# A fused attention and two-network kernel: the second network's first matrix two blocks at a time, in seven products instead of eight

## The chip, the cores and the metric

One Trainium2 chip, one core. The metric is the device time of one execution in microseconds (us). TensorE is called PE here, its weight loads PEld, VectorE is DVE, ScalarE is ACT, GpSimd is POOL, SyncE is SP.

## What is computed

```python
def _attn_ref(q, k, v):                 # [8, 8, 576, 64], chunks of 64
    scores = scale * np.matmul(q_c, k_c.transpose(0, 1, 2, 4, 3))
    scores = scores - np.max(scores, axis=-1, keepdims=True)
    attn = np.exp(scores)
    attn = attn / (np.sum(attn, axis=-1, keepdims=True) + 1e-09)
    out = np.matmul(attn, v_c)
...
def _moe_ref(x, w_gate, w_val, w_out, rms_g):      # first network, 512 -> 1536 -> 512
    xn = x / np.sqrt(np.mean(x * x, axis=-1, keepdims=True) + 1e-06) * rms_g
    g = xn @ w_gate
    silu = g * (1.0 / (1.0 + np.exp(-g)))
    return silu * (xn @ w_val) @ w_out
def _moe2_ref(x, w_in, w_out):                     # second network, 512 -> 2048 -> 512
    h = x @ w_in
    g = h * np.clip(h + 3.0, 0.0, 6.0) / 6.0
    return g @ w_out
```

The attention's output, 4608 tokens of 512 values, goes through the first network and then through the second. Everything is float32. The weights of both networks come as pairs of 32-bit words that are put together on the chip.

## The kernel before

The tokens form nine blocks of 512 columns (N), with the 512 features in four parts of 128 (KD = 4). For the matmuls each float32 operand is held as a high part, rounded to the PE's format, and a low part, the rest. A product of two operands is then three matmuls: high by high, low weight by high, high weight by low. The block of a network's input stands in XH and XL (high and low, four tiles of 128x512 each).

The first network runs block after block, 12 steps f each (FA). Between its matmuls two hooks issue other work: att_hook the attention of the block that comes next, prep_hook the preparation of weights. In blocks 1 to 8 of the first network, prep_hook takes four tiles of the second network's weights per block through Stash: load on ACT's queue, put together and split in high and low (ACT, DVE, POOL), store to DRAM on ACT's queue. In the last block all 32 tiles are fetched on SP's queue into the pool wp, 36 buffers of 128x2x512, where they stay. The first network's output goes to DRAM as well (yd, one tensor per block).

The second network, again block after block, has 16 steps f (FB) per block. A step has 12 matmuls of mm_up (L598), which make 128 rows of h in one PSUM bank, then relu on ACT (L813), gate on DVE (L814), split_act (the cast on ACT, L636, and the subtraction on POOL, L637), and 12 matmuls of mm_down_b (L615, L616, L619) with the activations of the step before into four PSUM banks. So the elementwise work of a step lies beside the matmuls of the next. At a block's start load_x2 brings the next block's input from yd in one 1 MB DMA (L661), and ahead of the last mm_down_b x_split splits it (casts L587 on ACT, subtractions L589, two on DVE and two on POOL). o_store (L651, L657) drains the four banks, ACT and DVE in turn, and writes them out.

The order of the instructions on each engine is the order in which the program issues them (manual_schedule); waits come from the tiles' dependencies and from how many buffers a pool has: 4 for tmp, 2 each for ah, al and st, 1 each for sg and xf.

Of the kernel before, what the change touches and what calls it, by code (L numbers as in the profile page):

```python
# [43 lines left out]
def fused_kernel(  # L44
# [20 lines left out]
    N = 512  # L65
# [4 lines left out]

    const = ctx.enter_context(tc.tile_pool(name="const", bufs=1))
# [123 lines left out]
    class Stash:  # L195


        def __init__(self, piece):
            self.piece = piece
            self.d = dr_p.tile([128, 2, 512], F32, name=f"stash_{piece[0]}{piece[1]}")  # L200

        def load(self):
            t = st_p.tile([128, 1024], U32, tag="st", name="sraw")
            o = t if self.piece[0] == "out2" else t.rearrange("p (k f) -> p k f", k=KD)
            nc.scalar.dma_start(out=o, in_=w_src(*self.piece))
            t = t.rearrange("p (n w) -> p n w", w=2)
            self.lw, self.hw = t[:, :, 0], t[:, :, 1]
# [10 lines left out]
        def split(self):  # L218
# [6 lines left out]
            self.lo = tmp_p.tile([128, 512], F32R, tag="tmp", name="slo")  # L225
            nc.scalar.copy(self.c.bitcast(F32R), self.lw.bitcast(F32))
            nc.gpsimd.tensor_tensor(self.lo, self.lw.bitcast(F32), self.c.bitcast(F32), op=ALU.subtract)

        def store(self):
            nc.scalar.dma_start(out=self.d[:, 0, :], in_=self.c.bitcast(F32))  # L230
            nc.scalar.dma_start(out=self.d[:, 1, :], in_=self.lo.bitcast(F32))

        def fetch(self):
            w = wp.tile([128, 2, 512], F32R, tag="w", name="w")
            nc.sync.dma_start(out=w.bitcast(F32), in_=self.d)
            W[self.piece] = w
# [344 lines left out]
    XH = xn_p.tile([128, KD, N], F32R, name="XH")  # L581
    XL = xn_p.tile([128, KD, N], F32R, name="XL")
# [9 lines left out]
    def mm_up(bank, w, xs):  # L592
# [19 lines left out]
    def mm_down_b(w, a, first, last, in_turn=False):  # L612
        def high(m):
            am = a[0][:, m * 128:(m + 1) * 128]
            nc.tensor.matmul(PS[:, YB + m, :], am, w[:, 0, :], start=first, stop=False)  # L615
            nc.tensor.matmul(PS[:, YB + m, :], am, w[:, 1, :], start=False, stop=False)  # L616

        def low(m):
            nc.tensor.matmul(PS[:, YB + m, :], a[1][:, m * 128:(m + 1) * 128], w[:, 0, :], start=False, stop=last)  # L619
# [27 lines left out]
    def o_store(b):  # L647
# [206 lines left out]
```

## Time and profile before

| | us |
|---|---|
| median of 3 runs | 1827.24 (1826.59 to 1827.74) |
| the profiled execution | 1826.32 |
| its span in the profile | 1824.5 |
| PE busy | 1766.5 (97% of the span) |
| DVE busy | 643.2 (35%) |
| ACT busy | 601.3 (33%) |
| POOL busy | 491.4 (27%) |

The span runs from the first to the last instruction of the profile; 1.8 us of the profiled execution lie around it. Up to about 84 us the attention of block 0 and the first weights are prepared, to 1036 us the first network runs, from 1036 us the second, with 87.04 us per block. Busy shares are means over all of it. What a group of instructions is worth is read in its own stretch.

### The profile page before, as it was taken

The page shows a single profiled execution, that of the slowest core. Times are in us where ns is not written, and L with a number is a line of the kernel's source. Part 1 is how long each engine was busy: PE and PEld are TensorE (multiplying, and loading weights), DVE is VectorE, ACT ScalarE, POOL GpSimd, SP SyncE. Part 2 cuts the span into 40 slices and gives each one's busy share as a digit, 9 for nine tenths or more (in the row PEclk, how much of TensorE's full clock was granted, in tenths as well). Part 3 has the DMA queues.
Part 4 walks back from the last instruction along what each step waited for, and adds up shares of the span by engine and source line. Part 5 has one row for each costly group of instructions (what it writes and reads, how often), then busy time and mean ns, then how long its engine had stood idle before and what let it go on. Part 6 is the DMA issues. An engine that isn't in the chain of part 4 may idle for free.

```text
span 1824.5 us, 24078 instructions
## 1 busy us (share of the span) xinstructions
PE 1766.5 (97%) x9856; PEld 1451.4 (80%) x9856; DVE 643.2 (35%) x858; ACT 601.3 (33%) x899; POOL 491.4 (27%) x359
## 2 busy tenths in 40 slices
PE   4689999999999999999999999999999999999998
PEld 4567788888888888888888888888888888888887
DVE  7886444454354445435432212121212121212111
ACT  5453333333333333333332223222323232223222
POOL 2321322232222223222222223232323232323222
PEclk7799999999999999999999999999999999999999
DMA  9831232323323242332237501010101010101000
GB/s 261 227 67 32 74 93 71 91 71 82 81 70 94 66 93 74 81 82 70 70 139 253 174 1 47 0 47 0 47 1 47 1 47 1 47 1 47 0 24 24
DMA packets 238000, 127.45 MB, mean 70 GB/s; under 512 B 193472, under 2 KB 213952, under 8 KB 236736
## 3 DMA queue, kind: packets, MB, share of 16 engines
q1 hardware_dynamic: 217920, 92.34, 19.4%
q10 hardware_dynamic: 19968, 33.56, 5.4%
q8 instruction: 77, 1.26, 0.3%
q14 instruction: 35, 0.29, 0.1%
HBM read 90.18 MB, written 35.65 MB: 69 GB/s over the span
## 4 chain that ended last, share of the span: by engine, by line
PE 91%; DVE 3%; DMA 2%; SPq 2%; issue 1%; ACT 1%; POOL 0%; DVEq 0%
PE PS L598 51%; PE PS L619 7%; PE PS L615 7%; PE PS L616 7%; PE PS L607 5%; PE PS L608 5%; PE PS L610 5%; PE PS L474 1%; DMA wraw<-in_moe_w_out_dram 1%; PE PS L534 1%; PE PS L516 1%; DVE kT L462 1%; SPq L265 0%; SPq L132 0%; DVE w L170 0%
## 5 line engine op out<-in xcount | busy, mean ns | idle before, releaser
L598 PE MATMUL PS<-XH,w 128*128 128x512 f32 x2880 | 721.5, 393 | 11.6 <-ACT sg L782 4.1
L637 POOL TENSOR_TENSOR al<-sg,ah 128x512 fp32r<-128x512 f32 x252 | 338.1, 1342 | 1216.1 <-ACT ah L636 1176.9
L598 PEld LDWEIGHTS PS<-XH,w 128*128 128x128 f32 x2880 | 543.2, 189 | 128.1 <-ACT sg L782 4.9
L598 PE MATMUL PS<-XL,w 128*128 128x512 f32 x1440 | 387.3, 391 | 0.0
L814 DVE SCALAR_TENSOR_TENSOR sg<-sg,PS 128x512 f32<-128x512 f32 x144 | 99.3, 689 | 635.5 <-ACT sg L813 635.5
L598 PEld LDWEIGHTS PS<-XL,w 128*128 128x128 f32 x1440 | 271.8, 189 | 57.9 <-POOL XL L400 0.6
L636 ACT CAST ah<-sg 128x512 fp32r<-128x512 f32 x252 | 156.3, 620 | 397.0 <-DVE sg L787 250.2
L813 ACT ACTIVATE sg<-PS,three 128x512 f32<-128x512 f32 x144 | 99.2, 689 | 452.5 <-PE PS L598 439.9
L616 PE MATMUL PS<-w,ah 128*128 128x512 f32 x576 | 224.1, 389 | 0.0
L615 PE MATMUL PS<-w,ah 128*128 128x512 f32 x576 | 224.1, 389 | 0.0
L787 DVE TENSOR_TENSOR sg<-sg,PS 128x512 f32<-128x512 f32 x108 | 74.2, 687 | 403.6 <-PE PS L598 399.6
L607 PE MATMUL PS<-ah,w 128*128 128x512 f32 x432 | 174.8, 405 | 0.0
L608 PE MATMUL PS<-ah,w 128*128 128x512 f32 x432 | 168.3, 390 | 0.0
L619 PE MATMUL PS<-w,al 128*128 128x512 f32 x576 | 154.4, 389 | 0.0
L619 PEld LDWEIGHTS PS<-w,al 128*128 128x128 f32 x576 | 108.1, 188 | 22.8 <-POOL al L637 0.4
L615 PEld LDWEIGHTS PS<-w,ah 128*128 128x128 f32 x576 | 108.1, 188 | 22.4
L616 PEld LDWEIGHTS PS<-w,ah 128*128 128x128 f32 x576 | 108.1, 188 | 22.4
L782 ACT ACTIVATE sg<-PS 128x512 f32<-128x512 f32 x108 | 64.6, 598 | 176.8 <-PE PS L598 159.8
L610 PE MATMUL PS<-al,w 128*128 128x512 f32 x432 | 115.6, 389 | 0.0
L607 PEld LDWEIGHTS PS<-ah,w 128*128 128x128 f32 x432 | 81.1, 188 | 18.8 <-issue 1.9
L608 PEld LDWEIGHTS PS<-ah,w 128*128 128x128 f32 x432 | 81.2, 188 | 17.5 <-issue 1.9
L610 PEld LDWEIGHTS PS<-al,w 128*128 128x128 f32 x432 | 81.0, 188 | 17.1 <-POOL al L637 0.3
(91 smaller groups left out, 1103.6 us busy)
## 6 DMA issues: line engine op xcount, KB each, us to landing
yd<-yst SPq DMA_DIRECT2D x18, 512.0 KB, 3.4
xf<-yd SPq DMA_DIRECT2D x9, 1024.0 KB, 6.6
sraw<-in_moe_w_in_dram ACTq DMA_DIRECT2D x16, 512.0 KB, 4.6
sraw<-in_moe_w_out_dram ACTq DMA_DIRECT2D x16, 512.0 KB, 4.0
w<-stash_in SPq DMA_DIRECT2D x16, 512.0 KB, 4.6
w<-stash_out SPq DMA_DIRECT2D x16, 512.0 KB, 4.6
out_dram<-ost SPq DMA_DIRECT2D x16, 512.0 KB, 3.2
wraw<-in_moe_w_gate_dram SPq DMA_DIRECT2D x12, 512.0 KB, 5.5
```

The lines of the kernel that those rows point to most:

```text
L598: nc.tensor.matmul(ps, w[:, wi, c * 128:(c + 1) * 128], xs[c][xi], start=(i == 0), stop=(i == n - 1))
L607: nc.tensor.matmul(ps, wm[0], a[0], start=first, stop=False)
L608: nc.tensor.matmul(ps, wm[1], a[0], start=False, stop=False)
L610: nc.tensor.matmul(PS[:, YB + m, :], w[:, 0, m * 128:(m + 1) * 128], a[1], start=False, stop=last)
L615: nc.tensor.matmul(PS[:, YB + m, :], am, w[:, 0, :], start=first, stop=False)
L616: nc.tensor.matmul(PS[:, YB + m, :], am, w[:, 1, :], start=False, stop=False)
L619: nc.tensor.matmul(PS[:, YB + m, :], a[1][:, m * 128:(m + 1) * 128], w[:, 0, :], start=False, stop=last)
L636: nc.scalar.copy(hi, t)
L637: nc.gpsimd.tensor_tensor(lo, t, hi.bitcast(F32), op=ALU.subtract)
L787: nc.vector.tensor_tensor(s, s, PS[:, VB, :], op=ALU.mult)
L813: nc.scalar.activation(s, PS[:, bank, :], AF.Relu, bias=three)
L814: nc.vector.scalar_tensor_tensor(out=s, in0=s, scalar=6.0, in1=PS[:, bank, :], op0=ALU.min, op1=ALU.mult)
```

## The change

The second network's first matrix is applied to two blocks at a time. The four quarters of a 256-column part of w_in (its two halves of rows by two steps f) and the two blocks' inputs (two halves of rows by two blocks) form two 2x2 block matrices, and their product is made by the Strassen scheme in Winograd's form: seven products of quarters in place of eight, at the price of sums of quarters before and after.

- Weights. Stash now goes by pairs of steps (i, eight of them). Beside the four quarters in high and low it makes the scheme's four sums of quarters (sums, DVE, half tiles) and splits them too (halves: one cast on ACT, one subtraction on POOL, for each of the two tiles). It still does one pair per block of the first network, with 12 store DMAs in place of 8, on ACT's queue. The first matrix stays in DRAM in this form; only the 16 tiles of w_out are fetched into wp, in the first network's last block.
- Stream. The weights of w_in come from DRAM while they are used: Stream.ahead loads 512 KB tiles on SP's queue into six buffers that the attention has left.
- Block 0 keeps the old form, with streamed weights. Blocks 1 to 8 go in four pairs.
- First half of a pair: for each of eight groups i (two steps f), seven products of six matmuls (product, L704), and the down matmuls (L725, L726, L729) of the pair's first block for the group before. ACT copies the first product out of PSUM (L1000), DVE adds the others to it (seven adds, L1003 to L1025), ACT makes four relus (L959) and DVE four gates (L962). The first block's two results are split by split_act as before; the second block's two are kept, unsplit, in buffers that XH and XL used, and in four of wp.
- Second half of a pair: 16 times mm_down_b for the second block, each with split_act one step ahead. Between these stands x_fill for the next pair (the same generator runs in block 0 for the first pair): for each of two parts c, two 512 KB DMAs from yd into the one xf buffer, four subtractions on DVE (T1 to T4, L927), and seven casts on ACT (L932) and seven subtractions on DVE (L935) into the 14 tiles X of wp, issued two pieces per step f.

The core of the diff:

```diff
+    def halves(x, hi=None):
+        if hi is None:
+            hi = tmp_p.tile([128, 512], U32, tag="tmp", name="shi")
+        lo = tmp_p.tile([128, 512], F32R, tag="tmp", name="slo")
+        nc.scalar.copy(hi.bitcast(F32R), x)
+        nc.gpsimd.tensor_tensor(lo, x, hi.bitcast(F32), op=ALU.subtract)
+        return hi.bitcast(F32), lo.bitcast(F32)
+    class Stash:
...
+        def keep(self, parts, at):
+            for z, t in enumerate(parts):
+                nc.scalar.dma_start(out=self.d[:, at, z, :], in_=t.rearrange("p (o n) -> p o n", o=2))
...
+        def sums(self):
+            a = [[r.lw.bitcast(F32)[:, h * 256:(h + 1) * 256] for h in range(2)] for r in self.r]
+            u = [[r.hw.bitcast(F32)[:, h * 256:(h + 1) * 256] for h in range(2)] for r in self.r]
+            (s2, s1), (s3, s4) = u
+            tt = nc.vector.tensor_tensor
+            tt(s1, a[1][0], a[1][1], op=ALU.add)
+            tt(s2, s1, a[0][0], op=ALU.subtract)
+            tt(s3, a[0][0], a[1][0], op=ALU.subtract)
+            tt(s4, a[0][1], s2, op=ALU.subtract)
...
+    class Stream:
...
+        def ahead(self, n=1):
+            for i, k_ in self.order[self.n:self.n + n]:
+                t = at_p.tile([128, 2, 2, 256], F32R, tag=self.TAGS[self.n % 6], name="wq")
+                nc.sync.dma_start(
+                    out=t.bitcast(F32).rearrange("p a b c -> p (a b c)"),
+                    in_=stash[i].d[:, 2 * k_:2 * k_ + 2].rearrange("p a b c -> p (a b c)"),
+                )
+                self.t[i, k_] = t
+                self.n += 1
...
+    def product(bank, op, x):
+        i = 0
+        for wi, xi in ((0, 0), (1, 0), (0, 1)):
+            for c in range(2):
                 nc.tensor.matmul(
-                    ps, w[:, wi, c * 128:(c + 1) * 128], xs[c][xi], start=(i == 0), stop=(i == n - 1)
+                    PS[:, bank, :],
+                    op[:, wi, c * 128:(c + 1) * 128],
+                    x[xi][:, c, :],
+                    start=(i == 0),
+                    stop=(i == 5),
                 )
                 i += 1
...
+        def x_fill(b):
+            for j in range(7):
+                if j not in X:
+                    X[j] = [wp.tile([128, 2, N], F32R, tag="w", name="xo") for _ in range(2)]
+            for c in range(2):
+                x4 = xf_p.tile([128, KD, N], F32, tag="xf", name="x4")
+                nc.sync.dma_start(out=x4[:, 0:2, :], in_=yd[b][:, c:c + 3:2, :])
+                nc.sync.dma_start(out=x4[:, 2:4, :], in_=yd[b + 1][:, c:c + 3:2, :])
+                yield
+                x11, x21, x12, x22 = (x4[:, z, :] for z in range(4))
+                src = {B11: x11, B21: x21, B22: x22}
+                for j, p, m in ((T1, x12, x11), (T2, x22, T1), (T3, x22, x12), (T4, x21, T2)):
+                    src[j] = tmp_p.tile([128, N], F32, tag="tmp", name="xt")
+                    nc.vector.tensor_tensor(src[j], p, src[m] if m in (T1, T2) else m, op=ALU.subtract)
+                    if j == T2 or j == T4:
+                        yield
+                for j in range(8):
+                    if j < 7:
+                        nc.scalar.copy(X[j][0][:, c, :], src[j])
+                    if j > 0:
+                        hi, lo = X[j - 1]
+                        nc.vector.tensor_tensor(
+                            lo[:, c, :], src[j - 1], hi[:, c, :].bitcast(F32), op=ALU.subtract
+                        )
+                    yield
+        def go(steps, n):
+            for _ in range(n):
+                if next(steps, True):
+                    return
...
+        prev = None
+        fill = x_fill(1)
+        for f in range(FB):
+            bank = GB + f % 2
+            i, z = divmod(f, 2)
+            low, top = ((0, 0), (2, 0)) if z == 0 else ((3, 0), (3, 1))
+            w2 = (stream.t[i, low[0]][:, low[1]], stream.t[i, top[0]][:, top[1]])
+            mm_up(bank, lambda wi, c: w2[c // 2][:, wi, c % 2 * 128:(c % 2 + 1) * 128], xs)
+            if z == 1:
+                stream.ahead(3)
+            s = sg_p.tile([128, N], F32, tag="sg", name="sg")
+            relu(s, PS[:, bank, :])
+            gate(s, PS[:, bank, :])
+            a = split_act(s)
+            if f > 0:
+                go(fill, 2)
+            if prev is not None:
+                mm_down_b(W["out2", f - 1], prev, f == 1, False)
+            prev = a
+        go(fill, 99)
+        mm_down_b(W["out2", FB - 1], prev, False, True)
+        o_store(0)
+        for b in range(1, NB, 2):
+            base = 0 if b % 4 == 1 else 4
+            yb = 4 - base
             prev = None
-            if b + 1 < NB:
-                load_x2(b + 1)
+            for i in range(NQ):
+                f0, f1 = 2 * i, 2 * i + 1
+                t = [stream.t[i, k_] for k_ in range(4)]
+                p0, p1, p2, p3 = (PS[:, base + z, :] for z in range(4))
+                add = nc.vector.tensor_tensor
+                product(base, t[0][:, 0], X[B11])
+                u1 = temp("u1")
+                nc.scalar.copy(u1, p0)
+                product(base + 1, t[0][:, 1], X[T2])
+                u2 = temp("u2")
+                add(u2, u1, p1, op=ALU.add)
+                product(base + 2, t[1][:, 1], X[T3])
+                u3 = temp("u3")
+                add(u3, u2, p2, op=ALU.add)
+                product(base + 3, t[1][:, 0], X[T1])
+                c22 = temp("c22")
+                add(c22, u3, p3, op=ALU.add)
+                r22 = g_tile(f1)
+                relu(r22, c22)
+                add(u2, u2, p3, op=ALU.add)
+                product(base, t[2][:, 0], X[B21])
+                add(u1, u1, p0, op=ALU.add)
+                r11 = sg_p.tile([128, N], F32, tag="sg", name="sg")
+                relu(r11, u1)
+                product(base + 1, t[3][:, 1], X[T4])
+                gate(r22, c22)
+                add(u3, u3, p1, op=ALU.add)
+                r21 = at_p.tile([128, N], F32, tag="sqs", name="r21")
+                relu(r21, u3)
+                product(base + 2, t[2][:, 1], X[B22])
+                stream.ahead(4)
+                gate(r11, u1)
+                add(u2, u2, p2, op=ALU.add)
+                r12 = g_tile(f0)
+                relu(r12, u2)
+                if prev is not None:
+                    for z in range(2):
+                        mm_down_b(W["out2", f0 - 2 + z], prev[z], i == 1 and z == 0, False, base=yb)
+                gate(r21, u3)
+                gate(r12, u2)
+                prev = [split_act(r11), split_act(r21)]
+            fill = x_fill(b + 2) if b + 2 < NB else iter(())
+            nx = []
+            for z in range(2):
+                mm_down_b(W["out2", FB - 2 + z], prev[z], False, z == 1, base=yb)
+                nx.append(split_act(g_tile(z)))
+            o_store(b, yb)
             for f in range(FB):
-                bank = GB + f % 2
-                mm_up(bank, W["in2", f], xs)
-                s = sg_p.tile([128, N], F32, tag="sg", name="sg")
-                nc.scalar.activation(s, PS[:, bank, :], AF.Relu, bias=three)
-                nc.vector.scalar_tensor_tensor(
-                    out=s, in0=s, scalar=6.0, in1=PS[:, bank, :], op0=ALU.min, op1=ALU.mult
-                )
-                a = split_act(s)
-                if prev is not None:
-                    mm_down_b(W["out2", f - 1], prev, f == 1, False)
-                prev = a
-            if b + 1 < NB:
-                x_split(xf.pop(b + 1))
-            mm_down_b(W["out2", FB - 1], prev, False, True, b == NB - 1)
-            o_store(b)
+                if 0 < f < FB - 1:
+                    nx.append(split_act(g_tile(f + 1)))
+                go(fill, 2)
+                last = f == FB - 1
+                mm_down_b(W["out2", f], nx[f], f == 0, last, last and b + 2 >= NB, base=base)
+            go(fill, 99)
+            o_store(b + 1, base)
 = ["q", "k", "v", "moe_w_gate", "moe_w_val", "moe_w_out", "moe_rms_g", "moe2_w_in", "moe2_w_out"]
```

Three places show what moves. On PE, a step of the second network before (XH and XL are the input, w a weight tile, ah and al the split activations), the row of L615 and L616 four times over:

```order
L598 MATMUL PS<-XH,w 128x512 x8
L598 MATMUL PS<-XL,w 128x512 x4
L615 MATMUL PS<-w,ah 128x512
L616 MATMUL PS<-w,ah 128x512
...
L619 MATMUL PS<-w,al 128x512 x4
```

And a group of the first half of a pair now (xo is an X tile, wq a streamed weight tile); the rows from the first L725 to L729 stand twice in a group:

```order
L704 MATMUL PS<-xo,wq 128x512 x42
L725 MATMUL PS<-w,ah 128x512
L726 MATMUL PS<-w,ah 128x512
...
L729 MATMUL PS<-w,al 128x512 x4
```

Two steps of 24 matmuls each for two blocks, 96 in all, are now 42 matmuls of products and 24 of down here, and 24 of down in the second half: 90.

On ACT, the end of a block of the second network and the start of the next before (xf is the next block's input, ost the drained output):

```order
L813 ACTIVATE sg<-PS,three 128x512 [waits PE_49,Pool_49]
L636 CAST ah<-sg 128x512 [waits DVE_49]
L587 CAST XH<-xf 128x512 [waits DMAHW4_49]
L587 CAST XH<-xf 128x512 x3
L651 ACTIVATE ost<-PS 128x512 [waits DMAHW2_49,PE_49]
L651 ACTIVATE ost<-PS 128x512 [waits DMAHW3_49,PE_49]
L813 ACTIVATE sg<-PS,three 128x512 [waits PE_49]
L636 CAST ah<-sg 128x512 [waits DVE_49]
L813 ACTIVATE sg<-PS,three 128x512 [waits PE_49,Pool_49]
L636 CAST ah<-sg 128x512 [waits DVE_49]
```

And the start of the second half of the first pair now (gx is a kept result of the second block, x_10170 the x4 buffer, xt the differences T1 to T4, xo the X tiles):

```order
L761 ACTIVATE ost<-PS 128x512 [waits DMAHW3_49,PE_49]
L746 CAST ah<-gx 128x512 [waits PE_49,Pool_49]
L932 CAST xo<-x_10170 128x512 [waits DMAHW6_49]
L746 CAST ah<-gx 128x512 [waits PE_49,Pool_49]
L932 CAST xo<-xt 128x512 [waits DVE_49]
L932 CAST xo<-xt 128x512
L746 CAST ah<-gx 128x512 [waits PE_49,Pool_49]
L932 CAST xo<-xt 128x512 [waits DVE_49]
L932 CAST xo<-x_10170 128x512
L746 CAST ah<-gx 128x512 [waits PE_49,Pool_49]
L932 CAST xo<-x_10170 128x512 [waits DMAHW7_49]
```

Before, the four casts of the next input stand in one place behind the block's last split, and nothing but the block's end is behind them. Now the fill's casts stand between the casts of the down matmuls' activations, so each ah cast is behind those fill casts that precede it and behind what they wait for, a DMA or DVE.

On DVE, around the end of a block of the second network before:

```order
L814 SCALAR_TENSOR_TENSOR sg<-sg,PS 128x512 [waits Activation_49] x16
L589 TENSOR_TENSOR XL<-xf,XH 128x512 [waits DMAHW7_49,PE_49,Activation_49]
L589 TENSOR_TENSOR XL<-xf,XH 128x512 [waits PE_49,Activation_49]
L651 TENSOR_SCALAR ost<-PS 128x512 [waits DMAHW5_49,PE_49]
L651 TENSOR_SCALAR ost<-PS 128x512 [waits DMAHW6_49,PE_49]
L814 SCALAR_TENSOR_TENSOR sg<-sg,PS 128x512 [waits Activation_49] x16
```

And the start of the second half of the first pair now:

```order
L761 TENSOR_SCALAR ost<-PS 128x512 [waits DMAHW2_49,PE_49]
L761 TENSOR_SCALAR ost<-PS 128x512 [waits DMAHW3_49,PE_49]
L927 TENSOR_TENSOR xt<-x_10170 128x512 [waits DMAHW7_49,DMAHW6_49]
L927 TENSOR_TENSOR xt<-x_10170,xt 128x512 [waits DVE_49]
L927 TENSOR_TENSOR xt<-x_10170 128x512
L927 TENSOR_TENSOR xt<-x_10170,xt 128x512 [waits DVE_49]
L935 TENSOR_TENSOR xo<-x_10170,xo 128x512 [waits Activation_49]
L935 TENSOR_TENSOR xo<-xt,xo 128x512 [waits Activation_49] x3
```

Before, the gates of the next block are behind the two subtractions of the split. Now no gate stands behind the fill in the second half; the fill's first subtraction waits for both DMAs, and everything of the fill is behind it in order.

## Rows read from the trace of the kernel before

**Rows 1.** The page: busy time per engine; shares of the chain that ended last.

```profile
PE 1766.5 (97%) x9856; PEld 1451.4 (80%) x9856; DVE 643.2 (35%) x858; ACT 601.3 (33%) x899; POOL 491.4 (27%) x359
...
PE 91%; DVE 3%; DMA 2%; SPq 2%; issue 1%; ACT 1%; POOL 0%; DVEq 0%
```

**Rows 2.** Busy time by stretch: a first-net block, its last block, a second-net block.

```profile
core 0: us, PE busy (x) PEld busy (x) DVE busy (x) ACT busy (x) POOL busy (x), PEclk, DMA share, GB/s
...
309.86:416.23 106.37, 105.96 (x708) 86.93 (x707) 47.86 (x55) 38.33 (x53) 28.71 (x20) 1.00 0.32 80
...
938.00:1036.00 98.00, 98.00 (x434) 81.16 (x433) 24.07 (x34) 22.79 (x39) 26.27 (x19) 1.00 0.71 236
...
1210.32:1297.36 87.04, 87.04 (x385) 72.07 (x385) 15.29 (x21) 24.13 (x39) 23.99 (x19) 1.00 0.07 25
```

**Rows 3.** PE's waits from 84 us on: us in total, times, longest.

```profile
PE PS L474 <- DVE kT L462: 8.2, 8, 5.3
PE PS L598 <- DVE sg L787: 3.1, 1, 3.1
PE PS L598 <- ACT XH L587: 2.5, 4, 2.0
PE PS L598 <- ACT sg L782: 1.7, 1, 1.7
```

**Rows 4.** Chain of waits, 1200 to 1400 us: start, length, what was last.

```profile
1202.15 2.72 PE PS L598 x12
...
1210.32 5.44 PE PS L598 x24
...
1297.36 5.44 PE PS L598 x24
```

**Rows 5.** The page's groups: busy us, mean ns of one, idle before.

```profile
L637 POOL TENSOR_TENSOR al<-sg,ah 128x512 fp32r<-128x512 f32 x252 | 338.1, 1342 | 1216.1 <-ACT ah L636 1176.9
...
L814 DVE SCALAR_TENSOR_TENSOR sg<-sg,PS 128x512 f32<-128x512 f32 x144 | 99.3, 689 | 635.5 <-ACT sg L813 635.5
...
L636 ACT CAST ah<-sg 128x512 fp32r<-128x512 f32 x252 | 156.3, 620 | 397.0 <-DVE sg L787 250.2
L813 ACT ACTIVATE sg<-PS,three 128x512 f32<-128x512 f32 x144 | 99.2, 689 | 452.5 <-PE PS L598 439.9
```

**Rows 6.** DMA issues, from the page: xcount, KB each, us to landing.

```profile
w<-stash_in SPq DMA_DIRECT2D x16, 512.0 KB, 4.6
```

**Rows 7.** Line L589's own view, on DVE: duration ns min/median/max.

```profile
L589 DVE TENSOR_TENSOR XL<-xf,XH x34: 683/1374/1780, 191.7 to 1731.1; 128x512 fp32r<-128x512 f32 x34
```

**Rows 8.** Timeline 1117 to 1129 us, a block's end: start, length, instructions.

```profile
1120.55 3.07 DVE L589 TENSOR_TENSOR XL<-xf,XH 128x512 fp32r<-128x512 f32 x2 [1.21 <-PE PS L619]
...
1121.34 3.44 POOL L589 TENSOR_TENSOR XL<-xf,XH 128x512 fp32r<-128x512 f32 x2
...
1123.11 1.98 PE L598 MATMUL PS<-XH,w 128*128 128x512 f32 x8
1123.54 1.27 DVE L651 TENSOR_SCALAR ost<-PS 128x512 f32<-128x512 f32 x2
...
1125.37 0.73 SPq L661 DMA_DIRECT2D xf<-yd  x1
```

**Rows 9.** Line L661's own view.

```profile
DMA to landing us min/median/max: 6.2/6.6/7.3
```

**Rows 10.** PE's timeline, 100 to 135 us, with the idle time before in brackets.

```profile
101.35 2.11 PE L598 MATMUL PS<-XH,w 128*128 128x512 f32 x8 [1.67 <-ACT sg L782]
103.29 1.07 PE L598 MATMUL PS<-XL,w 128*128 128x512 f32 x4
...
116.58 2.52 PE L598 MATMUL PS<-XH,w 128*128 128x512 f32 x8 [3.13 <-DVE sg L787]
118.89 1.91 PE L598 MATMUL PS<-XL,w 128*128 128x512 f32 x4
```

**Rows 11.** Busy time by stretch: the 12 matmuls behind the longer stop, columns as above.

```profile
116.58:120.70 4.12, 4.12 (x12) 2.87 (x12) 4.12 (x9) 3.80 (x6) 3.44 (x1) 0.68 0.02 4
```

More of the change, by code (lines that the diff above doesn't have):

```diff
@@ L224, in split @@
             )
[L225 to L233, printed above, removed]
-            w = wp.tile([128, 2, 512], F32R, tag="w", name="w")
-            nc.sync.dma_start(out=w.bitcast(F32), in_=self.d)
-            W[self.piece] = w
+            self.hi, self.lo = halves(self.lw.bitcast(F32), self.c)
@@ L239, in fused_kernel @@
+    stash = [Stash(i) for i in range(NQ)]
     xf = {}
@@ L670, in fused_kernel @@
         a_pieces = [(kd, f) for f in range(FA) for kd in ("gate", "val", "out")]
-        b_pieces = [(kd, f) for f in range(FB) for kd in ("in2", "out2")]
         prep_a = Prep(a_pieces)
-        stash = [Stash(piece) for piece in b_pieces]
         first = [Att(i) for i in range(NTL)]
@@ L755, in prep_hook @@
                 some(8)
-            f, o = divmod(hk, 3)
             if b > 0:
-                def at(g):
-                    return stash[4 * (b - 1) + g // 2] if 0 <= g < 8 and g % 2 == 0 else None
-                if o == 0 and at(f - 4):
-                    at(f - 4).store()
-                if o == 0 and at(f - 1):
-                    at(f - 1).load()
-                if o == 2 and at(f - 2):
-                    at(f - 2).within()
-                if o == 2 and at(f - 3):
-                    at(f - 3).split()
-            if b == NB - 1 and 0 < hk <= len(stash):
-                stash[hk - 1].fetch()
+                stash[b - 1].step(hk)
+            if b == NB - 1:
+                z = hk - 1 if hk <= FB - 2 else hk - 14
+                if 0 <= z < FB and (hk <= FB - 2 or z >= FB - 2):
+                    stash[z // 2].fetch_out(z % 2)
+                if hk == 32:
+                    stream.ahead(6)
+        order = [(i, k_) for i in range(NQ) for k_ in (0, 2, 3)]
+        order += [(i, k_) for _ in range(NB // 2) for i in range(NQ) for k_ in range(4)]
+        stream = Stream(order)
         for b in range(NB):
@@ L779, in fused_kernel @@
             for f in range(FA):
-                mm_up(GB, W["gate", f], xs)
+                mm_up(GB, whole(W["gate", f]), xs)
                 s = sg_p.tile([128, N], F32, tag="sg", name="sg")
@@ L785, in fused_kernel @@
                 hk += 1
-                mm_up(VB, W["val", f], xs)
+                mm_up(VB, whole(W["val", f]), xs)
                 nc.vector.tensor_tensor(s, s, PS[:, VB, :], op=ALU.mult)
@@ new lines, in fused_kernel @@
+        X = {}
+        G = {}
+        def x_fill(b):
[23 more added lines that the diff above has]
+                    yield
@@ new lines, in temp, with relu, gate @@
+        def temp(name):
+            return tmp_p.tile([128, N], F32, tag="tmp", name=name)
+        def relu(r, h):
+            nc.scalar.activation(r, h, AF.Relu, bias=three)
+        def gate(r, h):
+            nc.vector.scalar_tensor_tensor(out=r, in0=r, scalar=6.0, in1=h, op0=ALU.min, op1=ALU.mult)
+        prev = None
[17 more added lines that the diff above has]
+            prev = a
```

95 lines of the change are left out of this document (80 added, 15 removed).

## The prediction

> **What bounds the kernel now.** First the shares: PE is busy for 97% of the span and holds 91% of the chain that ended last [rows 1]. Then the stretches: a block of the second network takes 87.04 us, and PE is busy for all of them at granted clock 1.00, while DVE works 15.29, ACT 24.13 and POOL 23.99 us [rows 2]. Then the waits: from 84 us on PE waits for the other engines only at lines of the first network and the attention, 15.5 us in all [rows 3]; the same view from 1036.3 us on has none. So in the second network the time is matmuls times the time of one. The chain gives it: from one block's first matmul to the next is 1297.36 - 1210.32 = 87.04 us for 384 matmuls, 226.7 ns each, 2.72 us for twelve [rows 4]. Whatever removes a matmul there gains 0.227 us, until another engine makes PE wait.
>
> **The matmuls removed.** A group of two steps for two blocks was 96 matmuls and is now 42 + 24 + 24 = 90. Six fewer, by 8 groups and 4 pairs, is 192, and 192 x 226.7 ns = **43.5 us**. The shapes are the same (128x512, a new 128x128 weight for each), so I take the price unchanged. That gives 1826.3 - 43.5 = 1782.8 us against the profiled execution, whose 1.8 us around the span stay.
>
> The Trainium skill's page "TensorE: Matmul & The Clock Gate", section "Back-to-back issue gap", gives a sustained spacing of about 131 ns for a matmul of 512 columns behind a weight load; by that figure the 192 would be worth 25 us. The rows show 226.7 ns over whole blocks of this kernel, and the measurement decides.
>
> **First half of a pair.** Per group PE has 66 x 226.7 ns = 14.96 us (9.52 us in the first, which has no down matmuls). DVE has 11 instructions; the gate with one PSUM operand takes 689 ns [rows 5], so 7.6 us. ACT has one copy, four relus and two casts, at most 7 x 0.69 = 4.8 us; POOL two subtractions at 1.34, 2.7 us [rows 5]. Each bank is drained at least one product (six matmuls, 1.36 us) before it is written again, where the drain takes 0.69 us behind its product, and the down matmuls need the results of the group before, 9.5 us old. I book 0 for waits here. What it would take to break that is a rival below.
>
> **The weight stream.** 2 MB per group of 14.96 us is 140 GB/s on SP's queue, in a stretch that ran at 25; the last block of the first network carried 236 GB/s with PE busy for all of it [rows 2]. A 512 KB load landed after 4.6 us in that crowd [rows 6]; here each has some 12 us from issue to first use. 0, with 0 to 5 us as bounds.
>
> **The preparation.** Per block of the first network there are two more casts (ACT, 1.3 us), two more subtractions (POOL, 2.7), four half-size adds (DVE, at most 4 x 1.37 by [rows 7] = 5.5) and four more DMA issues. In a block of 106.37 us DVE is idle for 58, ACT for 68, POOL for 77 [rows 2]. What is queued behind ACT's DMA issues is the next silu, and PE waits for that only through the one PSUM bank of the gate product; the issues wait for buffers whose DMAs are some steps old. I take 0; bounds 0 to 4 us, for PE did wait there elsewhere, 1.7 and 3.1 us, once each [rows 3].
>
> **Second half of a pair: the fill.** This is where the change makes a new wait. PE needs one ah cast every 2.72 us, and ACT's casts for the next pair's input stand between them, held by DVE's differences and these by the DMAs. On SP these DMAs stand behind the pair's first two output stores and ahead of the rest. Time is counted from the first down matmul of the second block (f = 0).
> - First part. In the old kernel the load of the next input leaves 2.3 us after the new block's first matmul, behind DVE's late drains (1125.37 against 1123.11) [rows 8]. Now no subtraction holds DVE up, so I take 1.8 us. Landing took 6.2 to 7.3 us for 1 MB [rows 9]; here two of 512 KB, 6.2: 8.0 us. Then T1 and T2 on DVE. One with two SBUF operands takes 0.68 us alone [rows 7], but two of them beside POOL's took 3.07 [rows 8], so a POOL subtraction in the way costs 0.85 each. Here one POOL subtraction is just ending: 8.0 + 1.37 + 0.3 = 9.7. Then ACT's T2 and T1 casts and the ah cast behind them, 3 x 0.62 [rows 5]: 11.6 us. PE wants it at f = 4, 4 x 2.72 = 10.9. Stall **0.7 us**.
> - Second part. Its DMAs wait for the one xf buffer, that is for DVE's tenth instruction (four differences, six subtractions): 8.3 + 6.8 alone + 4 POOL subtractions x 0.85 = 18.5. Landing 6.2: 24.7; T1, T2 1.37; T2's cast and the ah cast 1.24: 27.3. PE wants that at f = 9, 24.5 + 0.7 = 25.2. Stall **2.1 us**.
> - PE also runs slower behind a stop. One of 1.67 us left eight matmuls at 2.11 us in place of 1.98 [rows 8, 10], 0.13 more; one of 3.13 us made twelve take 4.12 in place of 2.72, at granted clock 0.68, between its two levels [rows 10, 11], 1.4 more. I take **0.4** for the 2.1.
>
> 3.2 us per pair, for the three pairs with a next one: 9.6 us. With L589's median on DVE (1.37 each, [rows 7]) it is some 5.6 more per pair; with DVE alone and a landing as that of a 512 KB load (4.6) it is nothing.
>
> **Block 0.** Its fill is issued behind the second step, its DMAs behind three stream loads: all 2.6 MB at 236 GB/s [rows 2] are 11.1 us, and 8.0 as above if the stream doesn't slow them. With the middle, 9.6, then T1 and T2 (1.37), the gate behind them on DVE (0.69) and its cast (0.62) it is 12.3 us after the second step's product, and the down matmuls want it at 10.9. Stall **1.4 us**, 0 to 2.9. The fill's second part has 10.9 us from its issue to the gate behind it, so I book none.
>
> **The sum.** 1826.3 - 43.5 + 9.6 + 1.4 = 1793.8; the profiled execution lies 0.9 us under the median, so I say **1795 us**.
>
> **The rivals.**
> - *The fill is hidden.* If the landings come in under 5 us, or POOL doesn't hold DVE, the stalls are 0 to 5 us in all: 1783 to 1788. For it speaks that the DMA engines are 7% busy there [rows 2]; against it that 1 MB never landed under 6.2 [rows 9]. Chance 0.17.
> - *The fill costs its full price.* Each DVE instruction at 1.52 (half of 3.07, [rows 8]) makes the two stalls 2.0 and 7.2; with 1.4 and 0.4 for the slowed PE it is 11 per pair, 33 for three, and block 0 2.9: 1819. Halfway to the forecast is 1807. Against it: POOL has one subtraction per 2.72 us there, not an unbroken row as in [rows 8]. Chance 0.22.
> - *Every stop slows PE.* If all seven stalls cost 1.4 us more, 10 us in place of 1.2, it is 1803 to 1804. The 1.67 us stop speaks against that [rows 10]. This is in the case before. The Trainium skill, page "TensorE: Matmul & The Clock Gate", section "Why this matters for your kernels", says that a gap of PE between bursts brings its clock back to half speed; the longer stop agrees (0.68), the shorter doesn't show it.
> - *DVE bounds the first half: slower.* A group's 11 DVE instructions would take PE's 14.96 us at 1.36 us each; that is the point from which it decides. At 1.52, the price beside POOL, a group is 16.7 us: 1.77 more in seven groups, 7.2 in the first, 19.6 per pair, 78 for four: 1826 - 43 + 78 + 11 = 1872. For it: the adds lie among POOL's and ACT's work, and four gates have both operands in SBUF, as L589 had. Against it: POOL works 2.7 us of 14.96, and the seven adds have one operand in PSUM, where the gate keeps to 689 ns with POOL in the same step [rows 5]. Chance 0.06.
> - *It cancels.* Stalls in both halves of some 43 us in all, within 0.2%. Chance 0.04.
>
> **How the numbers follow.** The forecast (stalls of 5 to 19 us, 1788 to 1802) has 0.51. The range takes in the hidden fill and the lower part of the full price, to 1809: 1784 to 1809, 0.8 together. About 0.2% (3.7 us) is what a measurement of this kernel can tell from no change; faster by more are the forecast, the hidden fill and the full price, 0.90; within it 0.04; slower 0.06.
>
> **What would show it.** In the new profile a group of the first half should last 14.96 us at clock 1.00 with no wait of PE; the second halves should be 43.5 us in the last pair and some 46.7 in the others, with PE waiting for ah (L746) twice, at f = 4 and f = 9, and ACT in turn for xt or xf; block 0 should have one wait, at its third down step. Wrong would be: waits of PE for DVE's adds, a group over 15 us, waits for wq, a first network longer than before, or matmuls that take other than 226.7 ns.

## The result and the profile after

The changed kernel takes 1796.36 us (median; 1795.78 to 1796.53) against 1827.44 in the same comparison: a ratio of 0.983 (95% interval 0.9813 to 0.9847), about 31 us less. The forecast was 1795 us, 1784 to 1809. The profiled execution took 1796.53 us, its span is 1794.7.

The page of the changed kernel, busy times and the shares of the chain that ended last, the lines that answer to [rows 1]:

```profile
PE 1729.3 (96%) x9664; PEld 1417.1 (79%) x9664; DVE 881.4 (49%) x1186; ACT 643.5 (36%) x971; POOL 495.1 (28%) x359
...
PE 86%; DVE 6%; DMA 4%; issue 1%; SPq 1%; ACT 1%; POOL 0%; DVEq 0%; POOLq 0%
```

PE has 192 instructions fewer (9856 to 9664) and 37 us less busy time. DVE has 238 us more, and 5% of the chain went from PE to DVE and DMA. So there is a saving of matmuls, and something that was not there before.

The stretches say where. First the chain of waits in the second network: 84 product matmuls in a row are the first two groups of a pair, so each such row is a pair's start (start, length, what was last):

```profile
1123.69 19.04 PE PS L704 x84
...
1291.40 19.04 PE PS L704 x84
1459.59 19.04 PE PS L704 x84
1627.07 19.04 PE PS L704 x84
```

84 matmuls take 19.04 us, 226.7 ns each, as in [rows 4]. From pair to pair it is 167.71, 168.19 and 167.48 us, where 720 matmuls at that price are 163.2: 4.5, 5.0 and 4.3 us are lost, 13.8 in all. Then busy time by stretch (columns as in [rows 2]): nearly the whole first half of the first pair, and most of the last pair's second half, where no fill runs:

```profile
1123.53:1239.00 115.47, 115.47 (x511) 95.63 (x510) 58.86 (x90) 38.18 (x58) 20.21 (x16) 1.00 0.47 155
...
1742.00:1790.00 48.00, 48.00 (x213) 39.62 (x212) 1.83 (x3) 11.53 (x19) 21.37 (x17) 1.00 0.06 23
```

Both are full, at granted clock 1.00. What is lost lies where the second half has a fill. PE's waits from 84 us on (us in total, times, longest) name it; in [rows 3] no down matmul of the second network waited:

```profile
PE PS L725 <- ACT ah L746: 10.7, 9, 1.5
...
PE PS L693 <- DVE sg L890: 3.2, 1, 3.2
```

Nine stops, three per pair. PE's timeline of the first pair's second half (f = 0 begins at 1243.2 us) shows them at f = 3, 4 and 9:

```profile
1252.39 0.50 PE L725 MATMUL PS<-w,ah 128*128 128x512 f32 x1 [0.86 <-ACT ah L746]
...
1256.72 0.50 PE L725 MATMUL PS<-w,ah 128*128 128x512 f32 x1 [1.30 <-ACT ah L746]
...
1272.02 0.50 PE L725 MATMUL PS<-w,ah 128*128 128x512 f32 x1 [1.32 <-ACT ah L746]
```

ACT's timeline of that stretch shows what each late cast stood behind:

```profile
1245.28 0.62 ACT L746 CAST ah<-gx 128x512 fp32r<-128x512 f32 x1 [1.12 <-PE PS L726]
1251.20 0.62 ACT L932 CAST xo<-x 128x512 fp32r<-128x512 f32 x1 [5.30 <-DMA x<-yd]
1251.72 0.61 ACT L746 CAST ah<-gx 128x512 fp32r<-128x512 f32 x1
1255.01 1.14 ACT L932 CAST xo<-xt 128x512 fp32r<-128x512 f32 x2 [2.67 <-DVE xt L927]
1256.05 0.61 ACT L746 CAST ah<-gx 128x512 fp32r<-128x512 f32 x1
...
1267.96 0.62 ACT L932 CAST xo<-x 128x512 fp32r<-128x512 f32 x1 [2.89 <-DMA x<-yd]
1270.83 0.62 ACT L932 CAST xo<-xt 128x512 fp32r<-128x512 f32 x1 [2.25 <-DVE xt L927]
1271.35 0.61 ACT L746 CAST ah<-g 128x512 fp32r<-128x512 f32 x1
```

ACT is idle for 5.30 us with a fill cast at its head that waits for a DMA, and behind it stands the ah cast that PE needs. After that it idles 2.67 us for DVE's T2, with the next ah cast behind. At f = 9 it is T2 of the second part. DVE, POOL and SP say when their part came (DVE first, then POOL, then SP's queue):

```profile
1252.58 1.67 DVE L927 TENSOR_TENSOR xt<-x 128x512 f32<-128x512 f32 x1 [8.33 <-DMA x<-yd]
1254.28 0.69 DVE L927 TENSOR_TENSOR xt<-x,xt 128x512 f32<-128x512 f32 x1
...
1260.72 2.37 DVE L935 TENSOR_TENSOR xo<-x,xo 128x512 fp32r<-128x512 f32 x2
...
1269.38 0.69 DVE L927 TENSOR_TENSOR xt<-x 128x512 f32<-128x512 f32 x1 [4.59 <-DMA x<-yd]
```

```profile
1252.41 1.29 POOL L747 TENSOR_TENSOR al<-gx,ah 128x512 fp32r<-128x512 f32 x1 [4.88 <-ACT ah L746]
```

```profile
1244.76 0.79 SPq L920 DMA_DIRECT2D x<-yd  x1
1245.60 1.26 SPq L921 DMA_DIRECT2D x<-yd  x1
...
1263.12 0.52 SPq L920 DMA_DIRECT2D x<-yd  x1
```

The second part's DMAs leave at 1263.12, 18.4 us after the first part's, when DVE has read the buffer for the last time (its tenth instruction, the second of the two at 1260.72, ends at 1263.1).

POOL has a share in how long two of the stops are. T1 of the first part started beside POOL's subtraction of 1252.41 and took 1.67 us, where T1 of the second part, with POOL idle, took 0.69; T2, its cast and the ah cast for f = 4 came that 1.0 us later. Beside further subtractions of POOL the ten instructions took 10.5 us, where ten undisturbed ones, some 0.61 us from start to start, would be 6.2, and the second part's DMAs left 4.3 us later by it. By these rows I estimate that without POOL the stop at f = 4 would be some 0.3 us and the one at f = 9 would not be there. No run took POOL's work away.

The nine stops are 10.7 us of idle time; the other 3.1 of the 13.8 are 0.3 at each stop. Half of that is overlap: in an unbroken row a matmul is 0.39 us long in the trace and the next one starts after 0.23, and at a stop the 0.16 us between count as busy. The other half are the matmuls just behind the stop: the step at f = 3 takes 3.03 us from its first start to its last end, the one at f = 2 (1248.65 to 1251.53) takes 2.88. So the account closes: 1826.32 - 43.5 + 13.8 = 1796.6, and the profiled execution took 1796.53. Two smaller differences offset one another: the second network starts 0.4 us later than before, and the end behind the last matmul is some 0.5 us shorter.

### The profile page after: what moved, and what is told of

It reads as the page before. It is cut to its first block, busy times and chain, and to the rows that moved or that the text cites. A ratio compares the mean times of both kernels' runs of the same rounds, so it can differ in the third digit from the quotient of the medians.

```text
span 1794.7 us, 24671 instructions
## 1 busy us (share of the span) xinstructions
PE 1729.3 (96%) x9664; PEld 1417.1 (79%) x9664; DVE 881.4 (49%) x1186; ACT 643.5 (36%) x971; POOL 495.1 (28%) x359
## 4 chain that ended last, share of the span: by engine, by line
PE 86%; DVE 6%; DMA 4%; issue 1%; SPq 1%; ACT 1%; POOL 0%; DVEq 0%; POOLq 0%
PE PS L693 32%; PE PS L704 17%; PE PS L725 6%; PE PS L726 6%; PE PS L729 6%; PE PS L717 5%; PE PS L718 5%; PE PS L720 5%; DMA x<-yd 2%; DVE xo L935 1%; PE PS L569 1%; PE PS L629 1%; DVE xt L927 1%; DMA wraw<-in_moe_w_val_dram 1%; PE PS L611 1%
## 5 line engine op out<-in xcount | busy, mean ns | idle before, releaser
L747 POOL TENSOR_TENSOR al<-sg,ah 128x512 fp32r<-128x512 f32 x156 | 213.7, 1370 | 1023.0 <-ACT ah L746 716.1
L693 PE MATMUL PS<-XH,w 128*128 128x512 f32 x1728 | 439.1, 397 | 9.3 <-DVE sg L890 3.2
L693 PEld LDWEIGHTS PS<-XH,w 128*128 128x128 f32 x1728 | 328.1, 191 | 81.9 <-DVE sg L890 3.9
L704 PE MATMUL PS<-xo,wq 128*128 128x512 f32 x1344 | 309.2, 389 | 0.0
L704 PEld LDWEIGHTS PS<-xo,wq 128*128 128x128 f32 x1344 | 252.3, 188 | 52.4
L725 PE MATMUL PS<-w,ah 128*128 128x512 f32 x576 | 225.2, 391 | 10.7 <-ACT ah L746 10.7
L693 PE MATMUL PS<-XL,w 128*128 128x512 f32 x864 | 233.6, 392 | 0.0
L726 PE MATMUL PS<-w,ah 128*128 128x512 f32 x576 | 224.2, 389 | 0.0
L746 ACT CAST ah<-sg 128x512 fp32r<-128x512 f32 x156 | 96.8, 621 | 293.1 <-DVE sg L890 249.4
L693 PEld LDWEIGHTS PS<-XL,w 128*128 128x128 f32 x864 | 164.2, 190 | 35.3 <-POOL XL L495 0.6
L729 PE MATMUL PS<-w,al 128*128 128x512 f32 x576 | 154.5, 389 | 0.0
L725 PEld LDWEIGHTS PS<-w,ah 128*128 128x128 f32 x576 | 108.1, 188 | 36.8 <-ACT ah L746 14.5
L729 PEld LDWEIGHTS PS<-w,al 128*128 128x128 f32 x576 | 107.8, 188 | 23.0 <-POOL al L747 0.6
L726 PEld LDWEIGHTS PS<-w,ah 128*128 128x128 f32 x576 | 108.1, 188 | 22.3
L1003 DVE TENSOR_TENSOR u<-u,PS 128x512 f32<-128x512 f32 x32 | 22.0, 688 | 156.7 <-PE PS L704 147.6
L717 PEld LDWEIGHTS PS<-ah,w 128*128 128x128 f32 x432 | 81.1, 188 | 18.8 <-issue 1.9
```

What stands on the lines that cost most here:

```text
L693: nc.tensor.matmul(ps, w(wi, c), xs[c][xi], start=(i == 0), stop=(i == n - 1))
L704: nc.tensor.matmul(PS[:, bank, :], op[:, wi, c * 128:(c + 1) * 128], x[xi][:, c, :], start=(i == 0), stop=(i == 5),)
L717: nc.tensor.matmul(ps, wm[0], a[0], start=first, stop=False)
L725: nc.tensor.matmul(PS[:, base + m, :], am, w[:, 0, :], start=first, stop=False)
L726: nc.tensor.matmul(PS[:, base + m, :], am, w[:, 1, :], start=False, stop=False)
L729: nc.tensor.matmul(PS[:, base + m, :], a[1][:, m * 128:(m + 1) * 128], w[:, 0, :], start=False, stop=last)
```

## The experiments

The theory after the result: the gain is 192 matmuls at 226.7 ns and nothing else, and what is given back comes from the order on ACT's queue alone: an ah cast behind a fill cast that waits. Rivals: DVE and POOL hold each other up in the second half (the fill's work itself); the preparation, the stream or DVE's work in the first half costs something that the waits don't show. The first four runs begin from the changed kernel and change one thing each.

**Eight products.** One product is issued twice.

```diff
                 product(base + 3, t[1][:, 0], X[T1])
+                product(base + 3, t[1][:, 0], X[T1])
```

> One of the seven products (the one with T1) is issued twice in a row into the same bank, so each group has 48 product matmuls as the old form had; 192 matmuls more in all. Theory (the gain is the matmuls alone, 226.7 ns each): 192 x 0.2267 = 43.5 us more than the changed kernel, 1796.4 + 43.5 = 1839.9 us, 1839 to 1841; that is 12 to 13 us slower than the kernel before, which is what the scheme's new work costs. Rival (part of the gain comes from elsewhere, as from the pairing or the streamed weights): less than 43.5 us more, under 1835.

Measured: 1840.98 us (1840.19 to 1842.07), 44.6 more than the changed kernel's 1796.36, where 43.5 were expected, and 1.0078 times the kernel before (1.0063 to 1.0093). A group's products are now 48 (PE's timeline; a row's length runs to the end of the last matmul, a little over 48 x 226.7 ns = 10.88):

```profile
1216.93 11.04 PE L704 MATMUL PS<-xo,wq 128*128 128x512 f32 x48
1233.25 11.04 PE L704 MATMUL PS<-xo,wq 128*128 128x512 f32 x48
```

The two starts are 16.32 us apart, that is 72 matmuls of 226.7 ns. PE's idle time for ah is 10.6 us, as in the changed kernel. So the gain is the product that was saved; without it the new form is 14 us slower than the old one.

**The fill's first DMAs early.** They are issued in group 6 of the first half, where the buffer is free. The fill's other pieces stand one place earlier by it.

```diff
                 stream.ahead(4)
+                if i == 6:
+                    fill = x_fill(b + 2) if b + 2 < NB else iter(())
+                    go(fill, 1)
...
-            fill = x_fill(b + 2) if b + 2 < NB else iter(())
```

> The first two DMAs of the fill are issued in the first half's group 6, some 25 us ahead of the second half; the fill's other pieces stand one place earlier, the work is the same. Theory (PE's stops are ah casts that stand behind fill casts waiting for DMAs): the stops at f = 3 and f = 4 go, and DVE's tenth instruction ends at about 12 us after f = 0 in place of 19.9, so the second part's data land at 18 and the stop at f = 9 goes as well: 13.7 us less, 1782.7 us, 1782 to 1785. Rival (DVE and POOL get in each other's way and hold up the low parts): the same work in the same 43.5 us, stops stay, 1792 to 1796. Rival (only the first part's landing goes): 1796.4 - 3 x 2.8 = 1788.

Measured: 1781.29 us (1780.15 to 1782.99), 0.9749 times the kernel before (0.9732 to 0.9765). The waits of PE from 84 us on are those of the first network alone:

```profile
PE PS L569 <- DVE kT L557: 8.2, 8, 5.3
PE PS L693 <- DVE sg L890: 3.1, 1, 3.1
PE PS L693 <- ACT XH L682: 2.2, 2, 2.0
PE PS L693 <- ACT sg L885: 1.9, 1, 1.9
```

And from pair to pair it is 163.20 us, the 720 matmuls and nothing else (chain of waits):

```profile
1123.99 19.04 PE PS L704 x84
...
1287.19 19.04 PE PS L704 x84
```

All nine stops are gone, the one at f = 9 too: SP's queue shows that the second part's DMAs now leave at 1254.51 us, 8.6 us sooner, since DVE could begin sooner.

```profile
1218.71 0.53 SPq L920 DMA_DIRECT2D x<-yd  x1
...
1254.51 0.53 SPq L920 DMA_DIRECT2D x<-yd  x1
```

This is the fastest version.

**The fill's casts late.** The first part's DMAs stay where they were; the pieces behind them, and the second part's DMAs (f = 9), stand later, where no cast has anything to wait for.

```diff
-                go(fill, 2)
+                go(fill, (1, 0, 0, 0, 2, 2, 2, 2, 2, 1, 0, 2, 2, 2, 2, 2)[f])
```

> The DMAs stay where they are, but the fill's pieces stand later in the program: one at f = 0 (the DMAs), none to f = 3, two each from f = 4 to f = 8, the second DMAs at f = 9, none at f = 10, two each from f = 11 to f = 15. Theory: no fill cast waits any more when ACT comes to it, no stop is left: 1782.7 us, 1782 to 1786. Rival (DVE and POOL in each other's way): as much overlap as before, stops stay, 1792 to 1797, or the next pair starts late by some us.

Measured: 1782.84 us (1780.80 to 1783.46), 0.9757 times the kernel before (0.9743 to 0.9772). Again no L725 is among PE's waits, and the pairs take 163.20 us. DVE's 22 instructions per pair, POOL's 16 and their overlap are all still there: the lengthened ones of DVE add up to some 9.8 us in the first pair's second half, 9.7 in the changed kernel (estimates from the two timelines). What ACT has at its head has changed. So the rival that DVE and POOL hold PE up by themselves falls with this run and the one before; what is left of it is the share in the stops' length that is estimated above.

**The fill's casts first.** In each step they stand ahead of the ah cast.

```diff
+                go(fill, 2)
                 if 0 < f < FB - 1:
                     nx.append(split_act(g_tile(f + 1)))
-                go(fill, 2)
```

> In each step of the second half the two fill pieces are issued ahead of the step's ah cast in place of behind it; nothing else changes. Theory: every ah cast stands behind two more fill casts, so the stops come a step earlier and are longer: at f = 2 (3.7 us), f = 3 (1.4), f = 8 (2.6), with slower matmuls behind them some 9 us per pair in place of 4.5: 1796.4 + 3 x 4.5 = 1810 us, 1804 to 1814. Rival (DVE and POOL in each other's way): the same work, 1795 to 1799.

Measured: 1803.88 us (1803.32 to 1806.48), 7.5 more than the changed kernel; expected were 13.6, with 1804 as the lower bound, so it lies just outside. The same work, one place further up in a queue, costs 7.5 us, which the rival doesn't allow. PE's idle time for ah is 14.6 us in place of 10.7; the rest is matmuls that ran slower behind the longer stops (below, in the last section). But the stops are two per pair, at f = 2 and f = 8, and not three; PE's timeline of the first pair:

```profile
1252.18 0.79 PE L725 MATMUL PS<-w,ah 128*128 128x512 f32 x1 [4.01 <-ACT ah L746]
...
1271.71 0.50 PE L725 MATMUL PS<-w,ah 128*128 128x512 f32 x1 [1.26 <-ACT ah L746]
```

The stop at f = 2 moves PE by so much that the next ah cast is in time. I had added stops that partly stand in for each other.

The other four kernels begin from the version with the early fill, which has no stops in the second network, and ask for the costs that I had booked at 0.

**More adds in the first half.** The adds into u2, u3 and c22 are issued four times each, or five times (9 or 12 more).

```diff
                 add(u2, u1, p1, op=ALU.add)
+                add(u2, u1, p1, op=ALU.add)
+                add(u2, u1, p1, op=ALU.add)
+                add(u2, u1, p1, op=ALU.add)
...
```

> On top of the kernel with the early fill: in each group of the first half three of DVE's adds are issued four times (the sums are the same each time), 9 instructions more, 20 in place of 11, 20 x 0.688 = 13.8 us of PE's 14.96. Theory (DVE has room until it fills a group): no price per group; only the first group (9.52 us of PE) is overrun, its bank is drained late and the second group waits 2 to 4 us, 8 to 16 us for four pairs: 1781.3 + 8 to 16 = 1789 to 1797 us. Rival (the adds' place in a chain of dependent adds sets the pace, not DVE's total): waits in all groups, over 1820 us.

> As the run with nine adds more, but the three adds are issued five times: 12 more, 23 in all, 23 x 0.688 = 15.8 us against PE's 14.96. Theory (a group of the first half becomes DVE's when its instructions fill 14.96 us): 0.9 us in each of seven groups and some 6 in the first, 12 per pair, 49 for four: 1830 us, 1822 to 1838, with PE waiting for DVE's adds. Rival (DVE's instructions still hide): under 1800 us.

Measured: 1829.61 us (1828.22 to 1832.15) with nine and 1889.36 (1885.79 to 1891.88) with twelve more. Both are far above what my theory gave, and in both PE waits in every group, 32 times. With nine there are two stops of this kind, one in every group and one at the start of each pair's second group (PE's waits, then its timeline of the first pair):

```profile
PE PS L704 <- DVE u L1012: 17.9, 32, 1.3
PE PS L704 <- DVE u L1023: 10.0, 4, 2.5
```

```profile
1131.66 1.65 PE L704 MATMUL PS<-xo,wq 128*128 128x512 f32 x6 [0.53 <-DVE u L1012]
1135.81 10.07 PE L704 MATMUL PS<-xo,wq 128*128 128x512 f32 x36 [2.50 <-DVE u L1023]
```

L1012 is the last of the adds from the third product's bank, and the six matmuls that wait are the seventh product, which writes the same bank. In a pair's first group DVE starts on the second product 2.99 us in (1125.80, with the pair's start at 1122.81), does eight adds some 0.73 us apart, and ends at 1131.6 (DVE's timeline):

```profile
1125.80 0.69 DVE L1003 TENSOR_TENSOR u<-u,PS 128x512 f32<-128x512 f32 x1 [1.96 <-PE PS L704]
...
1130.92 0.69 DVE L1012 TENSOR_TENSOR u<-u,PS 128x512 f32<-128x512 f32 x1
```

PE would have come to the seventh product at 1122.81 + 36 x 0.2267 = 1130.97. So the rival was right: with adds repeated in this place, the chain from the second product to the third one's bank sets the pace, before DVE's total fills a group. The waits that the profile counts are 31 of the 48 us that this kernel takes more than the one with the early fill; the rest I have not accounted for one by one. With twelve more it has ten adds there and PE waits 2.0 us in each group:

```profile
PE PS L704 <- DVE u L1014: 62.5, 32, 2.0
```

In the changed kernel there are two adds in that chain. The second ends 5.0 us after the first pair's start (1128.50 on DVE's timeline, 1123.53), against 8.16 when the seventh product comes: DVE has room, 3.2 us in this place and 7.4 per group.

**The preparation without the sums.** The scheme's sums, their casts and subtractions are left out, and quarters are stored a second time in their place, at earlier places in ACT's order; this kernel leaves out the scheme's sums and so computes something else.

```diff
-                self.sums()
+                self.keep((r[1].hi, r[1].lo), slice(3, 6, 2))
...
-                self.h = [halves(x.hw.bitcast(F32)) for x in r]
```

> On top of the kernel with the early fill: the scheme's four sums of weight quarters, their two casts on ACT and two subtractions on POOL are left out of each block of the first network; in their place the quarters themselves are stored a second time, so the DMAs' number and size stay (the second network then multiplies by wrong weights). Theory (the preparation hides): same time, 1780 to 1783 us. Rival (it costs something in the first network): up to 4 us less, 1777 to 1779, and a first network that ends sooner than with it.

Measured: 1783.48 us (1780.84 to 1784.57), 0.9767 of the kernel before (0.9752 to 0.9781), against 0.9749 with the sums. It is not faster, and PE's waits in the first network are the same four lines with the same lengths within 0.3 us. The sharper measure is the eight blocks in which the preparation runs, from the first matmul of the first network's second block to that of the second network (PE's timelines; before, then the changed kernel):

```profile
203.43 2.12 PE L598 MATMUL PS<-XH,w 128*128 128x512 f32 x8
...
1036.07 1.98 PE L598 MATMUL PS<-XH,w 128*128 128x512 f32 x8
```

```profile
203.85 2.11 PE L693 MATMUL PS<-XH,w 128*128 128x512 f32 x8
...
1036.49 1.98 PE L693 MATMUL PS<-XH,wq 128*128 128x512 f32 x8
```

That is 832.64 us before and 832.64 in the changed kernel, 832.66 with the early fill and 832.68 without the sums. So neither the sums nor the four further DMA issues, which this run kept, cost anything that can be measured; the 0.4 us by which the second network starts later come from ahead of the preparation.

**Half as much stream again.** Every second weight tile of the pairs is loaded twice.

```diff
-                nc.sync.dma_start(
+                for _ in range(2 if self.n >= 24 and self.n % 2 else 1):
+                    nc.sync.dma_start(
...
```

> On top of the kernel with the early fill: every second 512 KB weight tile of the pairs is loaded twice in a row, 3 MB per group in place of 2, 210 GB/s in place of 140. Theory (the stream hides, its tiles come early): no change, 1780 to 1786 us, no wait of PE for a weight tile in the pairs. Rival (the stream is close to its limit): PE waits in each group, 1790 us and more.

Measured: 1782.60 us (1781.14 to 1784.12), 0.9764 (0.9750 to 0.9779): no change, and no wait of PE in the second network. The first half ran at 220 GB/s, with PE full (columns as in [rows 2]):

```profile
1139.00:1239.00 100.00, 100.00 (x443) 82.83 (x442) 49.62 (x76) 32.48 (x48) 17.01 (x14) 1.00 0.65 220
```

With the normal stream the same stretch has 153. The stream has room.

## Why the prediction was right

- **The matmuls.** 43.5 us were forecast. The products go at 226.7 ns, a group of the first half lasts 14.96 us as worked out, and issuing a product again brought 44.6 us back. Right. The 131 ns that the Trainium skill gives (page "TensorE: Matmul & The Clock Gate", section "Back-to-back issue gap"), by which the gain would have been 25 us, isn't what this kernel's rows show, before or after.
- **First half, stream, preparation.** Booked at 0, and 0 they are: no wait in the first halves, room in the stream and in DVE. The slower rival (DVE at 1.36 us an instruction) had against it that adds with a PSUM operand keep their length. They did, 688 ns in this group of the changed kernel, one of them (1136.24) beside a subtraction of POOL. The gates with both operands in SBUF kept it too, but in the first groups, looked at one by one, POOL was idle while they ran but for 0.1 us, so they don't test that price:

```profile
L1003 DVE TENSOR_TENSOR u<-u,PS 128x512 f32<-128x512 f32 x32 | 22.0, 688 | 156.7 <-PE PS L704 147.6 <-ACT u L1000 9.1
...
L962 DVE SCALAR_TENSOR_TENSOR sg<-sg,u 128x512 f32<-128x512 f32 x32 | 22.0, 686 | 0.0
```

  What was wrong in it is the point from which it decides: I took DVE's total per group, and the runs with more adds show that a bank in the chain can decide sooner.
- **The fill.** The mechanism was the one forecast, ah casts behind fill casts that wait for a DMA or DVE, and so were two of its three places; the sum was short: 3.2 us per pair expected, 4.3 to 5.0 measured. At f = 4 I had 0.7 and at f = 9 2.1 with 0.4 for slower matmuls; measured were 0.9, 1.3 and 1.3 us of idle time at f = 3, 4 and 9 in the first pair, and 1.0 around them, about half of it slower matmuls. Two things were wrong. The wait at f = 3 was missed: I looked only at T1 and T2, but X's first cast waits for the first DMA as well, and the ah cast for f = 3 stands right behind it. By the forecast's own landing, 8.0 us, that ah is ready at 8.0 + 2 x 0.62 = 9.2, and PE wants it at 8.2; the first DMA came in at 8.0 (ACT's 1251.20, from 1243.2). And the second DMA was mis-sized: 9.4 in place of 8.0 (DVE's 1252.58), with 1.0 in place of 0.3 for POOL's subtraction in T1's way. The rest of that path held: DVE's ten instructions took 10.5 us (10.2 in the sum), and the second part's data were there 6.3 us after its DMAs left (6.2). The stop at f = 9 was smaller than forecast, as PE had been moved by more before it.
- **Block 0.** 1.4 us were forecast, none came. What was mis-sized is the landing behind the stream, 9.6 us. The timeline of SP's queue and of DVE:

```profile
1038.95 3.49 SPq L324 DMA_DIRECT2D wq<-stash_in  x3
1042.53 0.56 SPq L920 DMA_DIRECT2D x<-yd  x1
1043.14 0.60 SPq L921 DMA_DIRECT2D x<-yd  x1
```

```profile
1049.14 0.69 DVE L927 TENSOR_TENSOR xt<-x 128x512 f32<-128x512 f32 x1 [4.85 <-DMA x<-yd]
```

  The three stream loads began to leave at 1038.95, and two of them go into buffers that the first step had read, so they were ahead of the second step's product (its end: 1041.93); I had put all 2.6 MB behind that. T1 could start 7.2 us after it, and block 0 took 87.04 us (1036.49 to 1123.53), as before.
- **The sum.** The errors offset one another in part: 1.4 less in block 0, 4.2 more in the pairs, and the 0.9 us that I added because the profiled execution had lain under the median were not there this time (1796.53 against 1796.36). That the forecast met the time within 1.4 us is partly luck.
- **The hidden fill**, a rival, is what the kernel becomes when the DMAs are issued earlier: 1781.3 us, where that rival began with 1783. As the kernel was forecast, it did not come about.

## What to carry to other kernels

Where work for later is put between instructions that feed the bound engine, ask of each of them what stands right behind it in its engine's queue, and place it behind the time at which its data are there: ACT, behind whose casts PE waited, was idle for 64% of the span here, and a change of order alone took the stops away. A load whose buffer is free belongs ahead of the stretch that uses it; this one moved up cost nothing elsewhere and gave 15 us. To find room for more work on an engine, look at the bank or buffer that comes back first, not at the engine's busy share.

## What the hardware showed that was not expected

- A stop of PE had two prices. Behind the stops of 0.7 to 1.5 us the granted clock stayed at 1.00 and a step, from its first start to its last end, took 3.03 us in place of 2.88. Behind the longer ones of the run with the fill's casts first, 4.01, 3.38 and 3.54 us, the granted clock was 0.51, 0.56 and 0.60, near the lower of its two levels (1.2 of 2.4 GHz), in the stretches looked at; behind the first, eight matmuls took 3.43 us (1252.18 to 1255.61) in place of 1.81. This is that stretch (columns as in [rows 2]):

```profile
1252.18:1255.50 3.32, 3.32 (x8) 2.64 (x9) 3.10 (x4) 0.71 (x2) 1.28 (x1) 0.51 0.03 5
```

  In the run with nine more adds a stop of 2.50 us was followed by 0.84, over the 10.58 us to 1146.39. What decides between the two prices, no run here was made to show.
- DVE's subtractions of two SBUF operands took 685 ns with POOL out of the way and, in the changed kernel's second halves, 1.67 to 1.80 us beside POOL's subtraction; in the run with the casts late there are lengths between, from 1.12 us on. The Trainium skill, page "SBUF — State Buffer", section "Who interferes with whom", says that such a DVE instruction contends with one of POOL that reads SBUF, over ports that they share and that one of them holds alone. The lengths agree: what is added, 0.4 to 1.1 us, is less than one subtraction of POOL (1.29). Over ten instructions of the fill it cost DVE some 4.3 us (10.5 from T1's start at 1252.58 to 1263.1, where 6.2 would be undisturbed), which moved the second part's DMAs; with the fill's casts behind their data none of it reached PE.
